# A memory-recurrent attention with a gated MLP on one Trainium2 core: the orders of all engines written out, and the gated weights loaded in 36 parts

## The chip, the core and the metric

The kernel runs on one core of a Trainium2 chip. Five queues of instructions run side by side: TensorE (matmuls, with their weight loads), VectorE (DVE), ScalarE (ACT), GpSimd (POOL) and SyncE (SP), which here only issues DMAs. Sixteen DMA engines move data. The engines wait for each other on semaphores. The metric is the device time of one execution in microseconds (us).

## What is computed

The reference applies two kinds of layer in turn, twice, each on a layer norm of its input and added to it:

```python
x = x + _A_ref(_layernorm(x), mem0, Wq, Wk, Wv, Wo, 32)
x = x + _B_ref(_layernorm(x), W_gate, W_up, W_down)
x = x + _A_ref(...)   # the same weights again
x = x + _B_ref(...)
```

`x` has 2048 tokens of 448 numbers in bf16. Layer A cuts them into 64 segments of 32. Each segment is put behind 8 memory rows, and 16 heads of size 256 attend over the 40 rows; the memory rows see only the memory, and the output of the memory rows is the memory of the next segment. So the memory is a recurrence of 64 steps:

```python
for s in range(n_seg):
    h = concat([mem, xs]); q, k, v = h @ Wq, h @ Wk, h @ Wv
    p = softmax(mask(q @ k.T / 16)); o = (p @ v) @ Wo
    mem = o[:, :8]; outs.append(o[:, 8:])
```

Layer B is `h = relu(x @ W_gate) * (x @ W_up)`, then `h @ W_down`, with 1792 hidden numbers.

## The kernel before, in words

**Products of weights.** `weights` (L807) loads Wq, Wk, Wv and Wo in pieces, turns them with TensorE (`transposes`, L827) and multiplies them (`product`, L851): A holds Wq times Wk per head, B (tile `Bsb`) holds Wv times Wo. After that the weights of a head never appear singly. The first 64 of the 448 rows come as "tails" by `load_tails` (L821); for the first group of heads they are issued on ACT's DMA queue.

**The recurrence.** `chain` (L997) makes one step of the memory: the memory's columns `mT` times A (L1025), copies to `Usb`, turning by `Selm` or `Selr` (L1182), scores (L1205), softmax on DVE and ACT, a transpose of the probabilities (L1245), probabilities times rows (L1269, L1273), copies to `YTm`, times B (L1062), sum to `Osum` or `Ohi`, and back into columns (L1104, L1089, L1096). The second A layer runs its own recurrence 7 steps behind the first (`LAG`), in the same instructions. The memory rows of each step also go by DMA into the row tiles HR.

**The tiles.** Every four steps a tile of 128 tokens can be worked on (`tiles`, L1513): four groups of heads with scores (L1358, L1387), softmax, a DMA transpose of the probabilities (tile `Tx` from `Px`), times rows (L1269) and times B (L1425); then norms, a DMA transpose into `G`, the gated units (L1447), ReLU and product into `hG` (L1452, L1453) and the down product (L1465). Copies out of PSUM go to ACT or DVE (`copy_any`, L394; lines L399 and L402).

**Loads of the gated weights.** `glu_weights` (L921) cuts W_gate and W_up into 7 parts each of 224 KB and W_down into 6 (four of 224 KB, two of 336). `glu_part` (L938) adds five of them in each of the first four steps to SP's queue; each starts only after some operation of that step, named by a key.

**The order of the work.** Nothing is issued directly. `_Sched.add` (L85) records an operation: the engines that can do it, what it reads and writes, a cost. There are 9215 of them, 2537 on TensorE, each of one or several matmuls. `schedule` (L142) then runs a list scheduler with a clock of its own: TensorE takes its operations in the order that the table `ORDER` (L428) writes down, an index for each; for the other engines it takes what is ready first on that clock, and so it also chooses between ACT and DVE and picks the PSUM bank. Its constants (turn of the tile mode 95 ns, hand-overs of 33 to 100 ns, DMA issue, head and rate) stand at L61 to L72. Where that clock sees TensorE idle for over 700 ns, `filler` (L272) puts in matmuls of a tile of zeros (`warm`); the program has 92 of them in four places, 43 of them before the first real matmul. `emit` (L315) writes each engine's list out with the waits that it needs. So on the chip every engine has a fixed order; a late instruction holds up all behind it on its engine.

Each matmul carries a tile mode (0 for the full array, 1 for 128 by 32, 2 for 64 by 128, 3 for 128 by 64, 4 for 64 by 32).

## Time and profile before

| what | us |
|---|---|
| median of 3 runs | 1541.31 |
| lowest, highest | 1538.32, 1542.31 |
| the profiled execution, its own time | 1540.38 |
| its span, first to last instruction | 1538.6 |
| TensorE busy, of the span | 1507.7 |
| TensorE idle before the first real matmul | up to 5.59, with the 43 warm-up matmuls in it |
| DVE, ACT, POOL busy | 1128.5, 819.9, 59.2 |
| SP, DMA issues | 979 |

The profile is of one execution. A line of it names an engine, a source line, what is written and read, the number of instructions and their time; "idle before" is the time that the engine stood still ahead of it, and behind the arrow stands what ended that. "issue" there means that the engine waited for nothing that the profile shows. Where the engine named had long been done, it was another, often a DMA. Matmuls overlap, and their ends are modelled, so one is listed longer than the distance to the next.

### The profile page before, as it was taken

The page shows a single profiled execution, that of the slowest core. Times are in us where ns is not written, and L with a number is a line of the kernel's source. Part 1 is how long each engine was busy: PE and PEld are TensorE (multiplying, and loading weights), DVE is VectorE, ACT ScalarE, POOL GpSimd, SP SyncE. Part 2 cuts the span into 40 slices and gives each one's busy share as a digit, 9 for nine tenths or more (in the row PEclk, how much of TensorE's full clock was granted, in tenths as well). Part 3 has the DMA queues.
Part 4 walks back from the last instruction along what each step waited for, and adds up shares of the span by engine and source line. Part 5 has one row for each costly group of instructions (what it writes and reads, how often), then busy time and mean ns, then how long its engine had stood idle before and what let it go on. Part 6 is the DMA issues. An engine that isn't in the chain of part 4 may idle for free.

```text
span 1538.6 us, 85020 instructions
## 1 busy us (share of the span) xinstructions
PE 1507.7 (98%) x38578; PEld 1097.6 (71%) x38578; DVE 1128.5 (73%) x3271; ACT 819.9 (53%) x2306; POOL 59.2 (4%) x245
## 2 busy tenths in 40 slices
PE   9999999999999999999999999999999999999998
PEld 6576766667767777767767777777768677777766
DVE  8745668778877877677876878667877878767764
ACT  7744555455645556544555546454655555544443
POOL 1000000000000000000000000000000000000000
PEclk9999999999999999999999999999999999999999
DMA  8532010000101101001011101001001101011001
GB/s 246 164 82 55 17 22 15 21 16 20 22 12 24 26 19 23 18 21 21 22 20 24 29 11 29 18 19 25 21 19 24 23 18 28 18 16 27 14 15 30
DMA packets 112695, 49.84 MB, mean 32 GB/s; under 512 B 82504, under 2 KB 111440, under 8 KB 112336
## 3 DMA queue, kind: packets, MB, share of 16 engines
q1 hardware_dynamic: 112016, 44.14, 12.4%
q8 instruction: 304, 4.98, 1.3%
q14 instruction: 55, 0.45, 0.1%
q10 hardware_dynamic: 320, 0.26, 0.1%
HBM read 21.35 MB, written 1.84 MB: 15 GB/s over the span
## 4 chain that ended last, share of the span: by engine, by line
PE 91%; DVE 3%; DMA 2%; SPq 2%; ACT 1%; issue 1%; POOL 0%; DVEq 0%; POOLq 0%
PE psG L1425 16%; PE psG L1358 15%; PE psG L1447 11%; PE psC L1062 11%; PE psC L1025 9%; PE psG L1465 5%; PE psG L1025 4%; PE psG L1269 3%; PE psG L1387 3%; PE psC L1182 2%; PE psG L1062 2%; SPq L805 2%; PE psG L1182 1%; PE psC L1205 1%; PE psG L858 1%; PE psC L1269 1%
## 5 line engine op out<-in xcount | busy, mean ns | idle before, releaser
L1425 PE MATMUL psG<-Bsb,YT 128*128 128x448 bf16 x1344 | 288.8, 353 | 0.1
L399 ACT ACTIVATE Ug<-psG 64x128 bf16<-64x128 f32 (+2 forms) x422 | 150.1, 371 | 89.5 <-PE psG L1358 70.8
L1447 PE MATMUL psG<-G,glu 64*128 64x128 bf16 x5950 | 187.2, 216 | 3.0 <-DMA G<-xn 1.7
L1425 PEld LDWEIGHTS psG<-Bsb,YT 128*128 128x128 bf16 x1344 | 116.1, 97 | 100.2 <-issue 12.6
L1447 PEld LDWEIGHTS psG<-G,glu 64*128 64x128 bf16 x5950 | 174.0, 94 | 14.1 <-issue 8.0
L1062 PE MATMUL psC<-Bsb,YTm 128*32 128x448 bf16 (+2 forms) x3864 | 175.0, 333 | 0.0
L1358 PE MATMUL psG<-HT,A 64*128 64x128 bf16 x3232 | 173.1, 216 | 0.4 <-issue 0.3
L1025 PE MATMUL psG<-A,mT 64*32 64x448 bf16 x4312 | 169.2, 350 | 0.7 <-POOL mT L1153 0.4
L1025 PE MATMUL psC<-A,mT 64*32 64x448 bf16 x3528 | 152.2, 350 | 1.3 <-DVE mT L402 0.6
L1358 PE MATMUL psG<-HX,A 64*128 64x128 bf16 x2424 | 147.5, 216 | 0.0
L1062 PEld LDWEIGHTS psC<-Bsb,YTm 128*32 128x32 bf16 x3864 | 95.3, 97 | 59.8 <-DVE YTm L402 0.7
L402 DVE CAST YT<-psG 128x448 bf16<-128x448 f32 x154 | 93.5, 617 | 38.0 <-PE psG L1273 37.1
L402 DVE CAST Ug<-psG 64x128 bf16<-64x128 f32 (+2 forms) x259 | 106.4, 421 | 20.2 <-PE psG L1358 15.5
L1358 PEld LDWEIGHTS psG<-HT,A 64*128 64x128 bf16 x3232 | 114.9, 94 | 7.0 <-issue 4.3
L1452 ACT ACTIVATE hG<-psG 128x512 bf16<-128x512 f32 (+1 forms) x126 | 68.5, 544 | 95.4 <-PE psG L1447 90.2
L1025 PEld LDWEIGHTS psC<-A,mT 64*32 64x32 bf16 x3528 | 77.8, 92 | 53.7 <-DVE mT L402 2.7
L1079 DVE TENSOR_TENSOR Osum<-psC,Osum 32x448 f32<-32x448 f32 (+2 forms) x112 | 68.2, 609 | 64.6 <-ACT Osum L1077 62.0
L399 ACT ACTIVATE YT<-psG 128x448 bf16<-128x448 f32 x201 | 102.0, 541 | 17.8 <-PE psG L1273 17.3
L1025 PEld LDWEIGHTS psG<-A,mT 64*32 64x32 bf16 x4312 | 88.3, 92 | 20.2 <-issue 1.2
L1465 PE MATMUL psG<-glu,hG 128*128 128x448 bf16 x448 | 99.6, 353 | 0.6 <-DVE hG L1453 0.6
L1358 PEld LDWEIGHTS psG<-HX,A 64*128 64x128 bf16 x2424 | 93.1, 94 | 0.0
L1358 PE MATMUL psG<-l,A 64*128 64x128 bf16 x2709 | 91.2, 216 | 0.3 <-issue 0.2
(276 smaller groups left out, 2927.9 us busy)
## 6 DMA issues: line engine op xcount, KB each, us to landing
Bsb<-in_A_Wq_dram SPq DMA_DIRECT2D x6, 384.0 KB
Bsb<-in_A_Wk_dram SPq DMA_DIRECT2D x6, 384.0 KB
glu<-in_A_Wv_dram SPq DMA_DIRECT2D x6, 384.0 KB
Tsb<-Ohi SPq DMA_DIRECT2D x128, 7.0 KB
X<-in_A_x_dram SPq DMA_DIRECT2D x16, 112.0 KB
glu<-in_A_Wo_dram SPq DMA_DIRECT2D x4, 448.0 KB
out_dram<-X SPq DMA_DIRECT2D x16, 112.0 KB
glu<-in_B_W_gate_dram SPq DMA_DIRECT2D x7, 224.0 KB
```

The costliest lines, as they stand in the source:

```text
L399: return E.activation(out, i, ACT.Copy, scale=1.0 if scale is None else scale)
L402: return E.tensor_copy(out, i)
L1025: i = E.matmul(ub[v].ap()[32 * j:32 * j + 32, 0:D], lhsT=self.mT[rw, b, :], rhs=self.A[rw, b, a0:a0 + D], start=(b == 0), stop=(b == 6), t ...
L1062: x = E.matmul(bo.ap()[32 * j:32 * j + 32, 0:d1 - d0], lhsT=self.YTm[:, q, :], rhs=self.Bsb[:, chunks[q], d0:d1], start=(i == 0), stop=(i ...
L1079: s.add("dve", dv_cost(n), lambda E, e, j=j, a_=a_, part=part: E.tensor_tensor(a_, part(j), a_, ALU.add), r=[bo], w=w, part=(j, 0), **P)
L1182: i = E.matmul(view()[:, :, k, v], lhsT=self.Usb[:, o:o + 128], rhs=Sel[:, :].rearrange("p (c q) -> p c q", c=2), start=True, stop=True)
L1269: return E.matmul(ps[:, n * q:n * q + n], lhsT=HR[rows, KM + 128 * q:KM + 128 * q + 128], rhs=PT, start=True, stop=True, tile_position=(b, 0))
L1358: i = E.matmul(ub[v].ap()[:, 128 * n:128 * n + 128], lhsT=self.A[rw, b, a0:a0 + 128], rhs=HT[rw, b, :, 0:SEG] if b < 4 else HX[rw, b - 4, ...
L1425: i = E.matmul(bo.ap()[:, 0:D], lhsT=YT[:, c, :], rhs=self.Bsb[:, 14 * g + c, :], start=(g == 0 and c == 0), stop=(g == 3 and c == 13))
L1447: i_ = E.matmul(two[v].ap()[:, 128 * c:128 * c + 128], lhsT=self.Wgu[rw, b, f0:f0 + 128], rhs=G[rw, b, :], start=(b == 0), stop=(b == 6), ...
L1452: s.add("act", 169 + 0.84 * N, lambda E, e, dst=dst, z=two[0], N=N: E.activation(dst, z.ap()[:, 0:N], ACT.Relu), r=[two[0]], w=[("hG", i, ...
L1465: i_ = E.matmul(bk.ap()[:, 0:D], lhsT=hG[:, c, :], rhs=self.Wd[:, c, :], start=(c == 0), stop=(c == NFC - 1))
```

## The change

1. `schedule` no longer schedules. The clock, the costs' constants and the list scheduler are gone. `ORDER` is now one list of 9235 entries for all engines: entry `v` is operation `v // 5` on engine `v % 5`. `BANKS` (2667 entries) gives the PSUM bank of each allocation, `FILLS` the places, numbers, banks and modes of the filler matmuls: four places, 44 matmuls.
2. The 20 parts of the gated weights become 36: each of the 14 parts of W_gate and W_up is split in two halves of its columns (112 KB each), and W_down goes in two parts of 112 KB and six of 224. `glu_part` has ten keys a step for five.
3. The tails of the first group of heads, on ACT's queue, are loaded in two halves: 8 DMAs for 4.
4. Some costs that `add` records in `constants` change; nothing reads them any more, except that a filler still carries one.

The core of the diff, with the table cut:

```diff
     def schedule(self):
+        names = [b for p in self.pools.values() for b in p]
+        order = {e: [] for e in self.ENGS}
+        last = {b: () for b in names}
+        seq = []
+        bank = iter(BANKS)
         for o in self.ops:
             o.need_inc = False
+        for n, v in enumerate(ORDER):
+            o = self.ops[v // 5]
+            o.eng = self.ENGS[v % 5]
+            assert o.eng in o.engs
+            if n in FILLS:
+                seq.append(self.filler(o, n, names, last))
+                order["pe"].append(seq[-1])
             for h in o.alloc:
+                h.name = names[next(bank)]
+                for p in last[h.name]:
+                    o.deps.setdefault(p, True)
+                last[h.name] = ()
...
+    def filler(self, o, at, names, last):
+        n, b, mode = FILLS[at]
...
+        f.deps = {p: True for p in last[names[b]]}
         f.deps[self.still] = True
...
+FILLS = {1969: (12, 2, 0), 9083: (15, 0, 0), 9211: (7, 0, 0), 9217: (10, 0, 0)}
...
-        self.wd_parts = ((0, 2), (2, 4), (4, 7), (7, 9), (9, 11), (11, NFC))
+        self.wd_parts = tuple((c, c + 1) for c in range(2)) + tuple((c, c + 2) for c in range(2, NFC, 2))
...
-        def load_tails(src, g, slot, eng="sp"):
+        def load_tails(src, g, slot, eng="sp", hs=(0, 1)):
             for v in range(2):
-                c = 512 * (g + 4 * v)
-                dst, z = self.Wst[slot][64 * v:64 * v + 64, 3, :], src[0:64, c:c + 512]
+                c, lo, hi = 512 * (g + 4 * v), 256 * hs[0], 256 * hs[-1] + 256
+                dst, z = self.Wst[slot][64 * v:64 * v + 64, 3, lo:hi], src[0:64, c + lo:c + hi]
...
-                    if h == 0:
-                        load_tails(W, g, slot[0, i], "act")
+                    load_tails(W, g, slot[0, i], "act", (h,))
...
-                parts.append((self.Wgu[rw, k, :], z, 229376, f"{n}{k}"))
+                for c in range(2):
+                    q = slice(c * F // 2, c * F // 2 + F // 2)
+                    parts.append((self.Wgu[rw, k, q], z[:, q], 114688, f"{n}{k}{c}"))
...
-        for k in ("uTm1", ("m", "E0"), ("m", "PT"), ("YTm", 0, 28), ("HRt", 0, s.now + 1)):
+        for k in (("Usb", 1), ("Usb", 3), "uTm1", ("m", "E0"), ("m", "PT"), ("YTm", 0, 28), ("Hi", 0), ("Hi", 256), "mTm", ("HRt", 0, s.now + 1)):
```

Compared by operation, the new list of TensorE is a local shuffle of the old one: an operation stands 3.9 places from where it stood, on average, and 89 at most.

## The prediction

> **What bounds the kernel now.** I read the page's busy row first, then TensorE's own waits, then the stages, then the timeline at single waits.

> ```profile
> PE 1507.7 (98%) x38578; PEld 1097.6 (71%) x38578; DVE 1128.5 (73%) x3271; ACT 819.9 (53%) x2306; POOL 59.2 (4%) x245
> ...
> q8 instruction: 304, 4.98, 1.3%
> ```

> TensorE is the bound. Only 1538.6 - 1507.7 = 30.9 us of its span is idle, and the change leaves every matmul of the work in place. So an order can win at most the idle time, plus what hides inside "busy". The second row is instruction fetch: 304 transfers of 16 KB, each 0.013 x 16 x 1538.6 / 304 = 1.05 us long on one DMA engine.

> ```profile
> PE psG L1447 <- DMA G<-xn: 1.7, 2, 1.4
> PE psG L1269 <- ACT hG L1452: 1.6, 1, 1.6
> ...
> PE psC L1269 <- issue: 1.5, 1, 1.5
> PE psG L1269 <- ACT l L399: 1.4, 1, 1.4
> PE psC L1104 <- DVE Ohi L962: 1.3, 2, 1.0
> PE psG L1269 <- DMA Tx<-Px: 1.3, 1, 1.3
> PE psG L1447 <- ACT Ug L399: 1.3, 1, 1.3
> ...
> PE psG L1182 <- issue: 0.5, 1, 0.5
> ```

> These are TensorE's waits (total, times, longest). Idle over 0.15 us adds up to 26.2 us: 4.2 before 80 us, 13.1 from 80 to 330, 5.7 from there to 1470, 3.2 after. Three kinds stand there. **Late DMAs**: the two of G, 1.7 in all, then 1.6, 1.5, 1.4, 1.3 and 1.3; where ACT or "issue" is named I count a DMA, because the one named was done well before. At 654.05 (L1269) the ACT instruction named had ended at 653.12, and the instruction reads Tx, which a DMA transpose writes. Sum 8.8 us. **Missing instructions**: waits ended by "issue" in the middle of an operation that waits for nothing, 0.5 at 1137.83 and four of about 0.3, some 2 us:

> ```profile
> 1137.06 0.25 PE L1182 MATMUL psG<-Selm,Usb 128*128 128x64 bf16 x3
> 1137.83 0.26 PE L1182 MATMUL psG<-Selm,Usb 128*128 128x64 bf16 x3 [0.53 <-issue]
> ```

> Counting the instructions of TensorE in the trace, such breaks lie at the same place of a 256-instruction block (number 191 or 192). **Chains too short of cover**: TensorE waits for ACT or DVE to finish what it fed them; the rest after 80 us, about 11 us.

> A listed idle is smaller than the real loss. The 17 warm-up matmuls that run at 4.05 to 4.90 us start every 0.056 us, but each is listed 0.219 long, so each idle hides a further 0.16. From start to start, the operations that are late by over 0.2 us lose 40 us in all.

> **The change, part by part.**

> *Turns.* Between operations of different tile modes TensorE loses 0.05 to 0.13 us, 54.6 us in the whole trace, more than all long waits. Each entry v of the new ORDER is operation v // 5 on engine v % 5; twenty operations are new (4 tail loads, 16 weight parts), so the others can be matched one by one with the old list. Changes of mode: 576 in the old order, 574 in the new. Two less at 0.095: **-0.2 us**.

> *Cover.* For every TensorE operation I counted the TensorE work (medians of its rows) that each list puts between the operation that feeds it and itself, and set it against what lies between: 0.2 us from the last matmul to the reader, the reader's median duration, 0.045 per hand-over, 2.2 for a DMA (the earliest transposes land 2.2 to 2.3 after issue); the banks come from the new table. Examples (listed idle; work between, old and new):

> - 247.49 L1104, 1.03: 1.63 to 2.97
> - 232.9 L1025, 0.32: 0 to 0.76
> - 302.2 L1025, 0.32: 0 to 2.23
> - 184.4 L1205, 0.21: 0.23 to 1.42
> - 222.4 L1245, 0.41: 1.40 both
> - 289.2 L1182, 0.57: 0.68 to 0.64
> - 1486.5 L1245, 0.61: 1.57 both
> - 1525.2 L1465, 0.63: 0.79 to 0.76

> Operations short by over 0.2 us, old and new: 6 and 4 before 80 us, 50 and 37 from 80 to 330, 18 and 14 to 1470, 15 and 14 after. On the old ones the trace lost 1.0, 13.8, 3.0 and 6.2 us, so one is worth 0.17, 0.28, 0.17 and 0.41. The differences give 0.3 + 3.6 + 0.7 + 0.4: **-5.0 us**, between 0 (another wait is late next) and -9 (the shortfalls also become smaller: 44.7 to 30.2 us summed, of which the trace bore out 0.6).

> *Late DMAs.* 8.8 us are there. The split of the gated weights halves what a transpose can stand behind on the DMA engines, but only from 75 to 133 us, where the old parts are issued; two of the waits (90 and 121 us) lie there. For the others the new order must have moved transposes off the fetches. The table does not give them more room: operations fed by a DMA with under 2 us to spare are 11 in the old list and 22 in the new, under 3 us 44 and 54. The spare at the late ones was 5.4 us (654.05), 4.0 (188.00), 1.2 (157.6) and 0.7 (121), so spare alone does not decide; where the fetch falls does, and the diff does not show that. Between -8.8 and +6 (four more at 1.4). I take half: **-4.4 us**.

> *Instruction breaks.* 2 us; between -2 and +2, since new neighbours put other operations on the block ends. **-1.0 us**.

> [...]

> *The opening.* FILLS has no entry near the start; its first is entry 1969, beside operations that ran at 318 us. So the 43 warm-up matmuls go:

> ```profile
> 0.99 4.03 PE L303 MATMUL psC<-warm 128*128 128x128 bf16 x43 [0.99 <-DVE cvec L774]
> ...
> 5.59 0.49 PE L840 MATMUL psG<-ident,Bsb 128*128 128x128 bf16 x6 [0.58 <-DVE X L755]
> ```

> Of these, 29 fall into 0.90:4.05 (0.107 apart), the rest run 0.056 apart: half rate for 3.1 us, though the granted-clock column reads 1.00 throughout. They ran in a wait for weights, so they cost nothing, and they took that slow start off the real work. Without them the real work runs slow. From 5.59 to 9.0 it is about 2.5 us, so it costs up to 2.5 more. Against that: the waits of 0.8 at 7.38 and 0.3 at 9.0 take up 1.1, and the first operation starts earlier. Its last input is the second tail load (ACT's queue, issued 1.36, landed 5.50); split in two, its first half carries 32 KB instead of 64. The first tail landed at 4.16, so the gain lies between 0 and 1.3; I take 0.9. Sum 2.5 - 1.1 - 0.9: **+0.5 us**, between -1 and +2.5. A wait of 1.2 for Wv at 45.3 is a second cover; if the weights there came earlier it would be gone.

> [...]

> *Queues.* 4 more tail issues on ACT (0.6 each, 2.4 us up to about 5.7) end before ACT's first eviction of old (6.18), and the table gives the first four evictions to DVE. 16 more weight issues on SP at 0.51 are 8.2 us; from 70 to 140 us SP issues 34 DMAs in 22 us, so it has room. A transpose queued behind three issues of one step waits 1.5: between 0 and +1.5, **+0.2 us**. Bytes per step stay the same. Evictions move by 10 between ACT and DVE: nothing, as TensorE is the bound.

> *Sum.* -0.2 - 5.0 - 4.4 - 1.0 + 0.5 + 0.2 = -9.9. The profiled execution took 1540.4 (span 1538.6); the median of three runs is 1541.3, 0.9 higher. 1540.4 - 9.9 + 0.9 = **1531.4 us**.

> **The rivals.**

> - *All of it works*: late DMAs and breaks vanish and the cover gains 9: -8.8 - 2 - 9 + 0.7 = -19, 1522 us. For: the waits are few (under 20 with 10.8 us) and each can be moved. Against: the DMA-fed operations have less spare than before.
> - *No gain*: the waits go elsewhere. ACT and DVE are in frozen order too (DVE 73% busy), and one eviction late there stands ahead of all others. What cover wins is lost in new conflicts: 1538 to 1545, say 1541.
> - *Slower, by late transposes*: 22 instead of 11 with under 2 us of spare, each late one 1.4 us. If the fetches are not where the order assumes, late landings grow with it. From 4.0 + 0.7 over 1.4 = four more than before on (the cover's 5.0 with turns, less opening and queues, is -4.5) the change loses; twice the old number (six more) gives -4.5 + 8.4 = +4, and ten more +9.5: about 1548. For: the counts. Against: half of the late ones had 3 us and more.
> - *It does not do what it says*: the knowledge of fetches brings nothing (late DMAs and breaks as before): -4.5, 1537; this lies at the edge of the forecast and is counted with it.

> **How the numbers follow.** A measurement of this kernel tells 0.3% (4.6 us) from no change. Forecast (-4.6 to -14): 0.45. All works: 0.23. No gain: 0.18. Slower: 0.14. So faster 0.68, same 0.18, slower 0.14. The range leaves out the far ends of both outer cases: 1520 (all works, with the opening at -1 and no queue cost: -8.8 - 2 - 9 - 0.2 - 1 = -21) to 1544 (five more late landings: -4.5 + 7 = +2.5).

> **What would show it.** Right: TensorE's idle over 0.15 us falls from 26 to about 17 us, most of it between 200 and 330; L1104's 1.0 and L1025's waits for mT go; L1182, L1245 and L1465 in the last 60 us stay; the waits for Tx and G keep two or three of over 1 us; the first matmuls of L840 stand 0.107 apart and begin before 5.2 us; "issue" breaks go on at other places. Wrong: more than ten waits of over 1 us at L1269 and L1447; TensorE's matmul steps slow beyond 12 us; idle time the same but moved to ACT or DVE; or a total of mode turns that costs another amount than 54 us.

## The result, and the profile after

| | before | after |
|---|---|---|
| median, us | 1541.31 (7 runs) | 1558.09 (7 runs) |
| lowest, highest | 1538.32, 1547.41 | 1549.97, 1561.41 |
| the profiled execution, its own time | 1540.38 | 1558.09 |
| its span | 1538.6 | 1556.3 |

The ratio of after to before is 1.0098, with a 95% interval from 1.0068 to 1.0127; measured a second time, on another chip, it is 1.0130 (1.0096 to 1.0165). The forecast was 1531.4, so the sign was wrong.

In the code after, line numbers are 245 higher than before: L1514 there is L1269 (probabilities times rows), L1692 is L1447 (gated units), L1490 is L1245, L1270 is L1025, L1349 is L1104, L1084 is L840. From the page of after, the busy row and the row of instruction fetches:

```profile
PE 1508.1 (97%) x38530; PEld 1097.1 (70%) x38530; DVE 1127.3 (72%) x3284; ACT 820.6 (53%) x2297; POOL 58.0 (4%) x241
...
q8 instruction: 304, 4.98, 1.3%
```

TensorE is busy as long as before (1507.7), and there are as many fetches. But the figure of before holds 4.0 us of warm-up matmuls that after has not. So of the 17.7 us between the two profiled executions some 4 are longer busy time of the work itself (the clock, below, and the slow opening, where the first six matmuls are listed with 0.80 us for 0.49 before), and the rest is idle time. TensorE's waits in after (total, times, longest, in us):

```profile
PE psG L1514 <- DMA Tx<-Px: 9.3, 9, 2.2
PE psG L1084 <- DMA Bsb<-in_A_Wq_dram: 5.1, 2, 4.8
PE psG L1692 <- DMA G<-xn: 5.0, 4, 1.5
PE psG L1692 <- ACT Osum L1322: 2.4, 3, 1.2
PE psG L1692 <- DVE str L1480: 1.8, 1, 1.8
PE psC L1514 <- DMA PTr<-Pr: 1.7, 2, 1.0
...
PE psG L1514 <- DMA PTr<-Pr: 1.3, 2, 1.1
...
PE psC L1349 <- DVE Ohi L1207: 0.3, 1, 0.3
```

The 4.8 of L1084 is the start. All the others of over 1.0 us stand at L1514 and L1692, the two lines that read what a DMA transpose wrote, as the releasers Tx, G and PTr say. At the lines where ACT or DVE is named, the instruction named had mostly been done long before; they, too, read G. Before had 1.3 for Tx and 1.7 for G. The wait of 1.03 us at L1104 is gone: the longest at L1349 is 0.3. Waits of over 1 us at the two lines went from 6 to 12; the prediction had named more than ten as a sign that it is wrong. Behind the first real matmul, idle times over 0.15 us sum at these two lines to 10.7 us before and 30.3 after, and at all others to 13.9 and 7.8. So the orders did win what they were to win elsewhere, and lost more at the transposes.

**Where in time.** By the start of each step of the recurrence, after is 6.6 us ahead at step 0, 1.7 at step 1, 5.0 at step 10 (227.9 us against 232.9) and 3.1 at step 15 (319.5). Most of the 6.6 at step 0 is only its place in the list: it is gone one step later. From step 15 on after falls back: 5.0 behind at step 27, 10.2 at step 34, 13.1 at step 54, 17.7 at the end.

**A measure of the late transposes.** For each of the 206 transposes that TensorE reads, three moments can be read from the trace: when its data are ready, when it lands (the update of its semaphore), and when the last matmul ahead of its reader starts. I call the time from the first to the third its *cover*, and what the second is behind the third, where it is over 0.06 us, *late*. The sum of the late is 9.5 us before (14 transposes) and 30.4 after (38). Covers under 4 us: 6 before, 39 after; under 4.6 us: 22 and 59. From issue to landing they take 2.2 to 3.9 us before and 2.3 to 4.1 after (5 to 95 of 100; medians 2.8 and 2.9), so the DMAs are hardly slower: their readers stand nearer.

**What makes a transpose slow.** Sorted by when a fetch of instructions starts, counted from the issue of the transpose, means over both traces: no fetch near it, or one 2 us and more behind it, 2.3 to 2.6 us; a fetch at 0 to 0.5 us 3.0; at 0.5 to 1.0 3.2; at 1.0 to 1.5 3.7; at 1.5 to 2.0 3.9 us. I say that a transpose is *hit* where a fetch starts between 0.1 us before its issue and 1.9 us behind it. Of the 59 short covers of after, 32 are hit. One of them, on SyncE's queue and then on TensorE, in after (start, duration, line, operation):

```profile
595.68 3.13 SPq L1044 DMA_TRANSPOSE Tx<-Px  x2
598.85 1.25 SPq L1044 DMA_TRANSPOSE G<-xn  x1
```
```profile
596.97 0.23 PE L1490 MATMUL psC<-ident,Pm 128*128 128x128 bf16 x1
598.98 0.34 PE L1514 MATMUL psG<-Tx,l 40*128 40x128 bf16 x6 [1.77 <-DMA Tx<-Px]
```

The transpose issued at 595.68 lands at 598.93, and the view of the DMAs for this stretch has one instruction fetch, which starts at 595.80. The reader L1514 comes directly behind L1490 and stands for 1.77 us.

**The clock.** Behind two of the waits the granted clock falls. The transpose read at 325.65 us is late by 2.3; behind it, in the table of stretches of after (stretch, its length, busy time of PE, PEld, DVE, ACT and POOL, then the granted clock, DMA share, GB/s):

```profile
323.00:326.80 3.80, 1.55 (x52) 1.45 (x54) 2.04 (x6) 1.64 (x4) 0.00 (x0) 1.00 0.18 36
326.80:330.20 3.40, 3.40 (x69) 3.09 (x64) 1.82 (x4) 1.65 (x4) 0.00 (x0) 0.50 0.02 5
330.20:333.00 2.80, 2.80 (x31) 1.61 (x29) 2.04 (x9) 1.20 (x7) 0.00 (x0) 1.00 0.01 3
```

For 3.4 us TensorE's granted clock is 0.50. I put the cost at half of that time, 1.7 us, since TensorE is busy in all of it. It happens again at 599.8, behind the wait shown above (0.50 for 3.41 us), and not once in the trace of before, whose mean granted clock is 1.000.

### The profile page after: what moved, and what is told of

The parts are those of the page before. It is cut to its first block, busy times and chain, and to the rows that moved or that the text cites. A ratio compares the mean times of both kernels' runs of the same rounds, so it can differ in the third digit from the quotient of the medians.

```text
span 1556.3 us, 84947 instructions
## 1 busy us (share of the span) xinstructions
PE 1508.1 (97%) x38530; PEld 1097.1 (70%) x38530; DVE 1127.3 (72%) x3284; ACT 820.6 (53%) x2297; POOL 58.0 (4%) x241
## 3 DMA queue, kind: packets, MB, share of 16 engines
q8 instruction: 304, 4.98, 1.3%
## 4 chain that ended last, share of the span: by engine, by line
PE 85%; DVE 7%; DMA 5%; ACT 1%; issue 1%; SPq 1%; ACTq 0%; DVEq 0%; POOL 0%
PE psG L1670 14%; PE psG L1603 14%; PE psG L1692 11%; PE psC L1307 11%; PE psC L1270 7%; PE psG L1710 5%; PE psG L1270 3%; PE psG L1514 3%; PE psG L1102 2%; PE psG L1632 2%; PE psC L1427 2%; DMA Tx<-Px 2%; PE psC L1450 1%; PE psC L1514 1%; PE psG L1427 1%
## 5 line engine op out<-in xcount | busy, mean ns | idle before, releaser
L1670 PE MATMUL psG<-Bsb,YT 128*128 128x448 bf16 x1288 | 277.3, 353 | 0.0
L273 ACT ACTIVATE Ug<-psG 64x128 bf16<-64x128 f32 (+2 forms) x441 | 156.7, 370 | 88.9 <-PE psG L1603 72.2
L1692 PE MATMUL psG<-G,glu 64*128 64x128 bf16 x5838 | 184.6, 216 | 11.5 <-DMA G<-xn 5.0
L1307 PE MATMUL psC<-Bsb,YTm 128*32 128x448 bf16 (+2 forms) x4144 | 187.6, 333 | 0.9 <-issue 0.5
L1692 PEld LDWEIGHTS psG<-G,glu 64*128 64x128 bf16 x5838 | 172.6, 94 | 22.0 <-issue 7.9
L1670 PEld LDWEIGHTS psG<-Bsb,YT 128*128 128x128 bf16 x1288 | 111.1, 97 | 91.2 <-issue 9.5
L1270 PE MATMUL psG<-A,mT 64*32 64x448 bf16 x4424 | 173.7, 350 | 0.3 <-issue 0.3
L1270 PE MATMUL psC<-A,mT 64*32 64x448 bf16 x3416 | 152.8, 350 | 1.9 <-DVE Tr L1476 1.0
L1307 PEld LDWEIGHTS psC<-Bsb,YTm 128*32 128x32 bf16 x4144 | 102.5, 97 | 65.2 <-DVE YTm L276 2.3
L276 DVE CAST Ug<-psG 64x128 bf16<-64x128 f32 (+2 forms) x265 | 111.1, 429 | 23.1 <-PE psG L1603 18.9
L1324 DVE TENSOR_TENSOR Osum<-psC,Osum 32x448 f32<-32x448 f32 (+2 forms) x120 | 73.2, 610 | 68.7 <-ACT Osum L1322 65.9
L273 ACT ACTIVATE YT<-psG 128x448 bf16<-128x448 f32 x214 | 107.7, 540 | 20.5 <-PE psG L1518 18.2
L1270 PEld LDWEIGHTS psC<-A,mT 64*32 64x32 bf16 x3416 | 76.5, 92 | 53.8 <-ACT mT L273 3.0
L1270 PEld LDWEIGHTS psG<-A,mT 64*32 64x32 bf16 x4424 | 90.3, 92 | 22.0 <-ACT mT L273 1.9
L1698 DVE TENSOR_TENSOR hG<-hG,psG 128x512 bf16<-128x512 bf16 (+1 forms) x113 | 68.9, 617 | 39.3 <-ACT hG L1697 38.4
L1603 PE MATMUL psG<-l,A 64*128 64x128 bf16 x2919 | 97.2, 216 | 0.0
```

The lines of the kernel that those rows point to most:

```text
L273: return E.activation(out, i, ACT.Copy, scale=1.0 if scale is None else scale)
L276: return E.tensor_copy(out, i)
L1270: i = E.matmul(ub[v].ap()[32 * j:32 * j + 32, 0:D], lhsT=self.mT[rw, b, :], rhs=self.A[rw, b, a0:a0 + D], start=(b == 0), stop=(b == 6), t ...
L1307: x = E.matmul(bo.ap()[32 * j:32 * j + 32, 0:d1 - d0], lhsT=self.YTm[:, q, :], rhs=self.Bsb[:, chunks[q], d0:d1], start=(i == 0), stop=(i ...
L1324: s.add("dve", dv_cost(n), lambda E, e, j=j, a_=a_, part=part: E.tensor_tensor(a_, part(j), a_, ALU.add), r=[bo], w=w, part=(j, 0), **P)
L1603: i = E.matmul(ub[v].ap()[:, 128 * n:128 * n + 128], lhsT=self.A[rw, b, a0:a0 + 128], rhs=HT[rw, b, :, 0:SEG] if b < 4 else HX[rw, b - 4, ...
```

## The experiments

Theory A: late transposes carry the loss. It soon had two halves. A1: the new order of TensorE puts readers too near. A2: the new orders fit the fetches of a program with another number of instructions in front of the work, so that the fetches hit the short covers. Rivals: B, the 36 parts; C, the frozen orders of ACT, DVE and SyncE; D, the cold opening without warm-up matmuls (in after TensorE works at half rate until 9.3 us; in before the warm-up matmuls reach the full rate at 4.05). "Old orders" are the kernel before's own orders, banks and fillers, written down in the form of after's tables. All ratios are to runs of before on the same chip; the medians of before differ from chip to chip by up to 4 us (1541.3 to 1545.0), so ratios are compared rather than medians.

### 1. The parts without the orders

```diff
-ORDER, BANKS, FILLS   # of after
+ORDER, BANKS, FILLS   # of before; new parts and half tails where the old ones stood
```

> The orders, banks and fillers of the kernel before, written down as a table for all engines, with the 36 parts and the tails in halves put in where the old parts stood: the whole change without the new orders. Theory A (the new order of TensorE puts the readers of DMA transposes too close behind them: 39 instead of 6 have under 4 us from data ready to the operation ahead of the reader, and the late landings grow from 9.5 to 30 us): the loss goes with the orders, so 1541, 1538 to 1545. Theory B (the 36 parts and the 20 more DMAs hold up the transposes): the loss stays, 1552 to 1560. Theory C (frozen orders of ACT, DVE and SP): 1541 here too, since this order, too, is fixed on the chip.

1551.7 us, ratio 1.0045 (1.0025 to 1.0065): worse than A said. TensorE's waits name a reason, which is neither of Tx nor of G (late transposes sum to 10.6 us):

```profile
PE psC L1514 <- DMA HR<-Ohi: 4.5, 2, 3.9
```

Memory rows wait behind parts. Was it the number of the parts, or my places for them? The same kernel with the parts alone moved in SyncE's order, to the moments where after issues them:

> The first kernel of this study (old orders, 36 parts; ratio 1.0045) with the parts alone moved in SP's order to the moments at which after issues them; all other engines keep their order. Of the 8 us that the first lost in its trace, 4.1 were two waits for memory rows (HR) behind a part; in after the same waits take 0.8. If the places of the parts made these waits: 1540 to 1546, ratio 0.999 to 1.002. If 36 parts cost as such (20 more DMAs on SP and the rings): 1547 to 1553, ratio 1.003 to 1.006.

1542.4 us, ratio 1.0009 (0.9993 to 1.0025). So the places make these waits, and at the places that after has, 36 parts and half tails cost nothing that can be measured. B falls.

### 2. No reader waits for a transpose

```diff
-lhsT=..., rhs=G[rw, b, :]             # gated units, reads ("G2", g), ("G2h", g, 0), ("G2h", g, 1)
+lhsT=..., rhs=self.Bsb[rw, b, 0:128]
-PT[r0:r0 + L, 128 * p:128 * p + 128]  # probabilities times rows, reads Tx
+self.Bsb[r0:r0 + L, p, 0:128]
```

and the same for PT of the ride chain. With the new orders, and with the old ones:

> The kernel after, but the matmuls that read the turned tiles (Tx, G, and PT of the ride chain) read Bsb instead, in the same shapes; the transposes still run, nobody on TensorE waits for them. The product with the probabilities and the gated units are so computed from other data. Theory A: the 30 us of late landings go, and the two drops of the clock with them (3.4): 1558 - 30 = 1528, between 1522 and 1535, at or below the next kernel. Theory C: other waits carry the loss, 1545 to 1555. Theory B: the late transposes are the parts' doing, which this kernel can't tell from A.

> The orders of before (with the 36 parts), and the same readers on Bsb in place of the turned tiles, with the same part of the computation changed. Theory A: only the 9.5 us of late landings of before go: 1541 - 9 = 1532, between 1527 and 1537; the new orders without waits are 0 to 8 us faster than this. Theory C: this kernel is 10 us or more faster than the new orders without waits.

New orders 1526.3 us, ratio 0.9870 (0.9837 to 0.9903): 32 us under after (35 by the ratios), and no drop of the clock; the late landings and the two drops of after make 30.4 + 3.4 = 33.8. Its waits, behind that of the start:

```profile
PE psG L1632 <- DMA Tx<-Px: 1.5, 2, 0.8
PE psC L1307 <- issue: 1.1, 2, 0.8
PE psG L1427 <- DVE Usb L276: 0.8, 2, 0.5
```

L1632 waits for the place of Tx, not for its data. Old orders 1545.9, ratio 0.9999 (0.9979 to 1.0019), which missed 1532: its trace has the waits for HR of the first kernel,

```profile
PE psC L1514 <- DMA HR<-Ohi: 9.9, 2, 6.2
```

so only 5.8 of the first kernel's 1551.7 went. How far would the new orders lead without them? The medians differ by 19.6 us, of which these waits take 9.9 - 0.8 = 9.1. The old orders' trace also has 17 us at half clock in three stretches, two at these waits and one in the opening; where TensorE had work in them, they cost 3.4 to 5.8 us. That leaves some 4 to 7 us by the medians, and 1 to 3 by the two profiled executions (15.9 us apart); behind the 3400th matmul (180 us in the old orders, 166 in the new) the new orders gain only 2. So A holds for the whole of the loss, and C falls, since nothing but the waits for transposes was taken away. How much faster the new orders are without them, this pair shows only roughly.

### 3. The new order for TensorE alone

```diff
-ORDER   # 9235 entries, all engines
+ORDER   # after's entries of TensorE alone; schedule() of before chooses the rest
```

> The new order for TensorE alone; ACT, DVE, POOL, SP, the banks and the fillers are chosen by the list scheduler of before, with the 36 parts. Theory A: the short cover is a matter of TensorE's list, so the loss stays: 1550 to 1560. Theory C (the frozen orders of the other engines make the conflicts): 1535 to 1543. With 43 warm-up matmuls or so back at the start, a cold opening that costs more than 3 us would show as a first 80 us that are faster than those of after by as much.

1577.1 us, ratio 1.0188 (1.0143 to 1.0232): slower than after, and outside both ranges. The short covers (30 under 4 us) are in TensorE's list, as A said, and the late landings are about those of after (32 us); its trace has four drops of the clock for two; what else it loses stays open. The orders frozen for the other engines help the list, which is against C once more.

### 4. Another count of instructions in front

Each matmul has a weight load (38530 of each in after), and there are 304 fetches for TensorE's 77,885 instructions, one for each 256. So n matmuls are 2n instructions, and every later fetch falls 2n instructions earlier in the work. The traces show this: counted in TensorE's own instructions, matmuls in front included, the fetches of all 20 traces start at one place of the 256, on average at number 228 to 239, eight of ten within some 50 of it. The matmuls stand where TensorE waits for its first weights:

```diff
-FILLS = {1969: (12, 2, 0), 9083: (15, 0, 0), ...}
+FILLS = {41: (80, 0, 0), 1969: (12, 2, 0), 9083: (15, 0, 0), ...}
...
+w = 8 if at < 100 else 128     # the small ones: 8 columns
```

> The kernel after with 80 matmuls of 8 columns of the zero tile ahead of TensorE's first operation, where it waits for its first weights: 160 instructions more (each matmul has a weight load), so every fetch of TensorE's instructions falls 160 instructions earlier in the work, or 96 later counted to the next block of 256. In the trace of after, 59 transposes have under 4.6 us from data ready to the operation ahead of the reader, and in 31 of these a fetch starts between 0.1 us before and 1.9 us after their issue. Moved by 160 instructions along TensorE's own record, it is 12 to 14, and 8 to 10 for 88 to 104 the other way. Theory A2 (the new order does keep the fetches away from the short transposes, but for another count of instructions in front than this kernel has): late landings fall from 30 to under 15 us, the clock drops go, and the time is 1558 - 14 = 1544, between 1534 and 1549; against before 0.993 to 1.003. Theory A1 (the readers are simply too close, whatever the phase): 1553 to 1560, ratio 1.008 or more. A gain by a warmer opening would be under 3 us and all before 80 us.

> The same with 128 small matmuls: 256 instructions, a whole block, so the fetches fall where they fall in after. A control for the one with 80: the same opening, another phase. A2: late landings stay at 30 us, time 1553 to 1561 and ratio 1.007 to 1.013 (a longer wait before the first operation of up to 2 us, and a gain from the warmer clock of up to 3). If the warm opening makes the difference and not the phase, it is as fast as the one with 80.

> The kernel after with the 43 warm-up matmuls of before put back ahead of the first operation: undoes the part of the change that was named the opening (and moves the fetches by 86 instructions, for which the record of after gives 17 to 19 us of late landings, 22 at its own phase). The prediction's term for the opening was +0.5, from -1 to +2.5: so up to 80 us it wins 0.5 to 2.5, and with the phase 2 to 5 in all: 1551 to 1556, ratio 1.004 to 1.009. If the cold opening were a large part of the loss: 1545 or less.

> The kernel after with 43 matmuls of 8 columns in front: the same 86 instructions as the 43 warm-up matmuls that won 13 us, but done by about 2.3 us, so TensorE is as cold at its first operation as in after. Phase (A2): late landings 11 to 15 us, not 30, and the time of the kernel with the 43 warm-up matmuls, 1545, between 1541 and 1549, ratio 1.000 to 1.005. A warm opening: no gain, 1553 to 1560, ratio 1.007 or more.

> The kernel after with 64 warm-up matmuls of 128 columns, 128 instructions, half a block: another point of the curve between 86 (late landings 11.5 us) and 160 instructions (22.7). Phase: 10 to 18 us late, 1541 to 1552, ratio 1.000 to 1.007, with up to 1 us for the later first operation. If more warm-up is what helps, it is as fast as the one with 43 or faster.

> The kernel after, unchanged, beside before on one chip: the base for the kernels with matmuls put in front, which ran in other groups. Ratio 1.008 to 1.012 (1.0098 was measured); late landings 25 to 33 us again and the fetches in the same places if the phase is a fixed property of the kernel, and spread over 10 to 30 us if it is drawn anew in each execution.

| in front | instructions | median, us | ratio | short covers hit | late, us |
|---|---|---|---|---|---|
| none (after) | 0 | 1558.1 | 1.0098 (1.0068 to 1.0127) | 32 of 59 | 30.4 |
| none, again | 0 | 1564.0 | 1.0130 (1.0096 to 1.0165) | 31 of 60 | 32.7 |
| 43 warm-up | 86 | 1544.9 | 1.0018 (0.9996 to 1.0041) | 20 of 59 | 11.5 |
| 43 small | 86 | 1549.4 | 1.0039 (1.0021 to 1.0057) | 23 of 60 | 20.5 |
| 64 warm-up | 128 | 1555.7 | 1.0087 (1.0064 to 1.0110) | 20 of 57 | 20.7 |
| 80 small | 160 | 1556.3 | 1.0086 (1.0069 to 1.0103) | 16 of 58 | 22.7 |
| 128 small | 256 | 1562.9 | 1.0121 (1.0095 to 1.0148) | 32 of 59 | 33.5 |

Hits and late are of one profiled execution each. The rows of 80 and 64 missed (1544 and 1541 to 1552 were expected), that of 43 warm-up beat its 1551 to 1556. Late landings and drops of the clock carry the differences between the rows: taken off each profiled execution's own time (1539.8 to 1565.4 us), with 1.7 us for each 3.4 at half clock, they leave 1523 to 1530 in all seven, beside 1529.0 of the kernel without these waits. The row of 80 has five drops, 8.5 us. And the phase shows in the late landings of the transposes that are hit: in a separate count, which gives totals of 14 to 37 us, these are 26, 22 and 26 us with 0, 0 and 256 instructions, 6 and 12 with 86, 16 with 128 and 13 with 160, while those of the others stay at 6.5 to 11. So a whole block brings back the hits, the late landings and the time of after, and 86 instructions take away most of the loss, with the 43 warm-up matmuls and with 43 small ones. Small ones leave the opening slow: behind 80 of them the first six real matmuls are listed with 0.80 us, as in after with none, and behind the 43 warm-up ones of before with 0.49. The phase is also a property of the program: a second execution of after hits or spares the same transposes in 175 of 206 cases, 256 instructions in 166, 86 in 84. The example of above with 43 warm-up matmuls, on SyncE's queue and on TensorE; now the fetch starts 0.63 us before the issue:

```profile
583.68 2.51 SPq L1044 DMA_TRANSPOSE Tx<-Px  x2
586.24 1.26 SPq L1044 DMA_TRANSPOSE G<-xn  x1
```
```profile
586.11 0.23 PE L1490 MATMUL psC<-ident,Pm 128*128 128x128 bf16 x1
586.27 0.34 PE L1514 MATMUL psG<-Tx,l 40*128 40x128 bf16 x6
```

The transpose lands 2.32 us after its issue (3.25 in after), and the same reader behind the same L1490 doesn't wait.

D was the rival here. Up to step 0 the 43 warm-up matmuls win nothing (48.3 us against 47.9 in after, 49.0 with the small ones); their 19 us of lead over after grow between step 0 and step 39. What a warm clock does is at most the step from 1.0039 to 1.0018, whose intervals overlap.

Do the old orders care? The kernel with ratio 1.0009, with its 43 warm-up matmuls taken out:

> The old orders with the 36 parts at the new places (1542.4, ratio 1.0009), without the 43 warm-up matmuls: the opening part of the change alone, with its 86 instructions. Phase: the old order's readers have 5 us and more in most cases, and its record gives 5.5 to 9 us of late landings at any phase, so it stays at 1541 to 1547, ratio 0.999 to 1.004 (the opening itself up to 2.5). If the cold opening costs as such: 1550 or more.

1547.6 us, ratio 1.0026 (1.0009 to 1.0043), late 13.0 us where it had 8.5. So the same edit, 43 matmuls fewer, costs the old orders 0.17%, with intervals that overlap, and the new ones 0.8 to 1.1%.

### 5. More cover for the readers, and a mixture

```diff
-ORDER   # of after
+ORDER   # of after; 23 readers of transposes 1 to 13 places later, with what depends on them
```

> The kernel after with 23 readers of transposes (and what depends on them) moved back in TensorE's order by 1 to 13 places, so that they have up to 1.5 us more; the number of instructions is the same, so the fetches keep their phase but for these shifts. A1 and A2 both: some 10 of the 30 us of late landings go, 1545 to 1552, ratio 1.000 to 1.006. If something else than late transposes carries the loss: 1555 to 1562.

> The new orders throughout, with 37 waiting operations moved back (by a count that lets every transpose take 3.8 to 4.1 us), and 44 warm-up matmuls in front. With A: late landings from 30 to about 12 us, at a cost of some 17 more turns of the tile mode (1.6 us): 1558 - 18 + 2 - 1 = 1541, between 1536 and 1548, ratio 0.995 to 1.003. If moving readers only shifts the waiting to ACT's and DVE's results, as it did in the kernel with 23 moved (1557, late landings 20.5): 1551 to 1558.

23 moved: 1557.5 us, ratio 1.0091 (1.0072 to 1.0110), a miss. Late landings fell to 20.5 us, as expected, but the time hardly did (by nothing against the first measurement of after, 1.0098, and by 0.4% against the second, 1.0130, on the same chip): between 80 and 1475 us, TensorE's waits over 0.4 us that end with a transpose fell from 22.1 to 16.0 us in all, those for DVE, ACT and POOL rose from 3.0 to 5.7, and 17 more turns of the tile mode cost some 1.6 (at the 0.095 us that before's 576 turns lose on average). That leaves about 2 us of gain in the trace. 37 moved, with 44 warm-up matmuls: 1547.3, ratio 1.0041 (1.0020 to 1.0062), late 9.3, 21 more turns. Without late landings and drops of the clock the two profiled executions are at 1536 and 1538, against the 1523 to 1530 of the kernels with unmoved readers. So moving readers takes the late landings away, but costs some 10 us elsewhere, of which these waits and turns are a part; the rest I can't place.

New orders up to a step of the recurrence, old ones behind it:

```diff
-ORDER   # of after
+ORDER   # of after up to step 15 (320 us), then the rest in the order of before
```

> The new orders up to step 15 of the recurrence (320 us), the old orders from there on, with the 36 parts at the places that the new order gives them. By the start times of the steps, after is 3.1 us ahead of before at step 15 and loses 20 us behind it; before loses nothing there: 1541 - 3 to - 5 = 1536 to 1539, ratio 0.996 to 0.999, which makes it the fastest so far if A holds in place. If the 36 parts cost as in the kernel with the old orders (6 us), it is 1540 to 1545.

> The new orders up to step 15, the old ones behind it, as before in this study (1545.5, ratio 1.0021), with 16 waiting operations moved back in TensorE's order, and 86 matmuls of the zero tile ahead of the first operation (52 of 8 columns, 34 of 128), 172 instructions: there the record of that kernel puts its late landings at 3 us for this phase, where it puts 11.7 at its own and 16.5 were measured. By the late transposes (A with the phase): 9 us less of them, and 1 to 2 us by a warm opening: 1533 to 1538, ratio 0.994 to 0.998. If the phase and the nearness of readers are not what holds this kernel: 1543 to 1548, ratio 1.001 to 1.003.

> The new orders with the 43 warm-up matmuls up to step 44 of the recurrence (935 us), the old orders behind it. In the profiled run of the new orders with 43 warm-up matmuls TensorE is 8.7 us ahead of before at step 44 and loses 6 of them between steps 44 and 59; the old orders lose nothing there. So 1541 - 8.7 = 1532, between 1529 and 1539, ratio 0.992 to 0.999: a version that beats both. If the lead at step 44 was luck of that one run (its kernel's median is 6 us above it): 1538 to 1543.

> The new orders to step 44 with 43 warm-up matmuls and the old orders behind it (ratio 0.9994), with 27 waiting operations moved back in TensorE's order so that a transpose may take 3.8 to 4.1 us. By cover: late landings from 11.3 to about 6 us, no drop of the clock, at 14 more turns (1.3 us): 1532 to 1538, ratio 0.994 to 0.998, beside 0.9967 of the one with the new orders to step 15. If moved readers only shift the wait to others: 1541 to 1545, ratio 0.998 to 1.001.

| kernel | median, us | ratio | late, us |
|---|---|---|---|
| new to step 15 | 1545.5 | 1.0021 (1.0008 to 1.0034) | 16.5 |
| the same, 16 moved, 86 matmuls in front | 1536.7 | 0.9967 (0.9953 to 0.9980) | 4.7 |
| new to step 44, 43 warm-up | 1543.9 | 0.9994 (0.9976 to 1.0012) | 11.3 |
| the same, 27 moved | 1543.5 | 1.0001 (0.9987 to 1.0015) | 8.7 |

The first missed its 1536 to 1539. The second, as expected, is faster than before and after; it joins three edits (readers moved, another phase, warm-up matmuls), and no run separates them. In its trace no transpose lands later than 1.3 us behind the last matmul ahead of its reader, and the clock stays at 1.000 in all of its 12 runs, which lie between 1535.2 and 1538.2. TensorE's longest waits (this kernel's code is one line longer, so L1515 is L1514 of after; the wait of 1.8 is at a reader of memory rows, HR, and of no DMA transpose):

```profile
PE psC L1515 <- issue: 1.8, 1, 1.8
PE psG L1515 <- ACT hG L1698: 1.3, 2, 0.7
PE psC L1515 <- DMA PTr<-Pr: 1.1, 1, 1.1
PE psC L1271 <- DVE Tr L1477: 1.1, 1, 1.1
```

New to step 44 did not give the 1532 that the lead in one profiled run of the kernel with 43 warm-up matmuls promised; that run (1539.8) lay 5 us under its kernel's median. The two programs are the same up to step 44, yet their traces reach it at 925.9 and 937.6 us: the lead was largely the luck of that run. With 27 moved, the second rival's 1541 to 1545 came.

## Why the prediction was wrong

**Late DMAs: -4.4, measured +20.9** (9.5 to 30.4). This is the step that failed. It saw that operations fed by a DMA had less room (22 against 11 with under 2 us to spare, at a price of 2.2 us for a transpose), said that not the spare but "where the fetch falls" decides, and then took half of the old lateness as won, though no row showed where the fetches would fall. Two numbers were too kind. 2.2 is the fastest transpose; the half of them that a fetch hits takes 3.0 to 3.9, so the limit to count under was a cover of about 4 us: 6 before, 39 after. And of "four more at 1.4" there were 24 more, at 20.9 / 24 = 0.87 each.

**The opening: +0.5, right where it stood, wrong elsewhere.** The first matmul came at 4.75 us, 0.84 earlier (0.9 was taken), at half rate until 9.3 (0.80 us for the first six, 0.49 before), and at step 0 the warm-up matmuls make no difference; at its 100th real matmul after is 0.3 us behind. But the step priced 43 matmuls by their time alone. They are 86 instructions, so without them every later fetch falls elsewhere, and putting them back won 0.8 to 1.1% of the time; 43 small ones, which win nothing up to step 0 (49.0 us against 47.9), won 0.6 to 0.9%, some 9 to 14 us. For the fetches the prediction had only the breaks in TensorE's own stream (±2).

**Cover: -5.0, right in the main.** Idle times over 0.15 us outside the readers of transposes fell by 6.1 us behind the first matmul: by 1.9 before 80 us (waits for weights), 3.2 from there to 330, nothing to 1475 and 1.0 after, where the term had 0.3, 3.6, 0.7 and 0.4. L1104's wait went, those of L1025 for mT from ACT and DVE fell from 0.9 to 0.3 (though a new one of 1.0 stands at that line), those of L1245 stayed (0.6 and 0.6 before, 0.9 and 0.6 after).

**Turns -0.2, queues +0.2, breaks -1.0.** The late starts at changes of mode, each counted up to 0.13 us, sum to 65.1 us in both traces; the parts cost nothing measurable at their places. Waits named "issue" went from 3.6 to 2.1 us, but the difference is one of 1.5 that the prediction itself counted as a DMA. Without it, and without one of 2.3 at a reader of G in the kernel with 43 warm-up matmuls, they are 2.1, 2.1 and 2.3: the breaks moved and cost the same, and the gain of 1.0 did not come.

**The clock** was in no step: two drops, 3.4 us.

Together, for the profiled executions: 1558.1 - 1540.4 = 17.7 = 20.9 (late) + 3.4 (clock) - 6.6 for all the rest, which the prediction put at -5.5.

**The rivals.** *Slower, by late transposes* is what happened, with its own condition ("if the fetches are not where the order assumes"). It counted six to ten more late ones, about 1548; with the 24 and 0.87 its sum gives 1541.3 - 4.5 + 20.9 = 1557.7. That this is so near the measured 1558.1 is partly luck: the sum leaves out the clock's 3.4, and the rest won more than its 4.5. *Does not do what it says* is half true: the short covers of after are hit as often (32 of 59) as transposes in general (102 of the 222 issued), so what it may know of fetches is of no use in this program; with 86 instructions more it is 20 of 59.

**What stays open.** That the new orders were made for a program with about 86 more instructions in front is an inference from the table of section 4; between 86 and 160 instructions the late landings and the ratios do not follow the number of hits closely (20 of 57 hit and 1.0087 at 128), and single executions of one kernel lie up to 15 us apart. Why the clock drops five times in one kernel and once in another, and what moving readers costs beyond the waits and turns named, is not settled either.

## What to carry to other kernels

A reader of a DMA needs cover for the slow landing, not for the fastest (here 3.9 us with a fetch at the wrong moment, and 2.2): take the time from issue to landing of all transfers of the kind, and count the readers whose cover lies under the ninth of ten. Where an order was fitted to the instruction fetches of one program, any instruction added or dropped ahead of it moves all of them, as the 86 of the warm-up did here; a warm-up that costs nothing in its place can set the time of the whole kernel (putting it back won 0.8 to 1.1%). To find such a dependence, put a whole block of idle instructions in front (256 instructions here, ratio 1.0121 beside after's 1.0098 and 1.0130) and then a part of one (86, ratios 1.0018 and 1.0039): if the block changes nothing and the part does, it is the phase.

## What the runs showed of the hardware

**Behind a wait of 1.8 us the granted clock can be halved.** In all traces of this study together, start-to-start gaps of 1.75 to 2.0 us behind the opening were followed by 3.4 us at a granted clock of 0.50 in 8 of 25 cases, gaps of 2.0 to 2.5 in 9 of 20, longer ones in 11 of 11, and gaps of 1.0 to 1.75 in 1 of 181. Each drop of 3.4 us (3.41 in after) costs 1.7 by the estimate above, half of its length; three of the stretches were twice as long (6.83).
